# Windowed attention and a low-rank mixer on one core: an MLP in nine chunks of 512 tokens over all batches, attention in its slots

## The chip, the core and the metric

The kernel runs on one core of a Trainium2 chip. The core's engines run in parallel, each through its own queue of instructions in order: TensorE (PE; its weight loads are shown apart, as PEld) multiplies matrices into PSUM, eight banks of 512 float32 columns on 128 partitions; VectorE (DVE) and ScalarE (ACT) do elementwise work and empty PSUM; GpSimd (POOL) does elementwise work in SBUF and here issues all loads; SyncE (SP) issues the stores. Semaphores order the engines among each other. The metric is the device time of one execution in microseconds (us).

## What is computed

```python
# q, k, v: (8, 8, 576, 64) batch, head, token, dimension; U (576, 32), V (32, 576)
# w_ch1 (512, 2048), w_ch2 (2048, 512); all float32
scores = (q @ k.T) / 8, kept where 0 <= i - j < 64, else -1e9
attn   = softmax(scores)                       # per head
x      = attn @ v, heads side by side          # (8, 576, 512)
h      = x.T @ U @ V                           # mixes tokens through rank 32
u      = x + h.T
out    = u + relu(u @ w_ch1) @ w_ch2           # (8, 576, 512)
```

## The kernel before

The operands become bfloat16 in the loads; sums stay float32 in PSUM. Work goes batch by batch. In the attention of one batch (`attention_phases`) heads go in four pairs j, and the 576 tokens in nine blocks of 64, each of which sees 128 keys.

- **T(j)** (L168 to L211): k and q of a pair are transposed by TensorE, five tiles each, into two PSUM buffers (`tp`, pool `ps_sm`). ScalarE copies k into `kt` (L184, L188), VectorE copies q into the block-diagonal `qbd` (L204, L208), whose two halves hold the two heads.
- **S(j)** (L218 to L248): nine matmuls of 128 columns, three to a PSUM tile `sc`; exp on ScalarE (L237, 384 columns), multiplication by a 0/1 mask on VectorE (L243).
- **PV(t, hh)** (L255 to L289): for 128 tokens and four heads, eight matmuls of 65 columns: 64 of v and one of ones, which gives the softmax's sum. The even block of 64 tokens goes to the lower 64 PSUM partitions, the odd one to the upper. A block's 128 keys begin at a multiple of 64, so v is also held shifted by 64 tokens: `vaugB`, written by two VectorE copies (L165, L166) from the loaded `vaugA`. A reciprocal and a multiplication on VectorE (L282, L283) give x.
- **U** (hht, L297) and **V** (mix, L315): x against U, five accumulating matmuls of 512 columns with U padded to 128 columns, a copy on ScalarE (L309); then V against that, five matmuls, and the residual add on VectorE (L326) gives u. Then u is transposed (L341, L344).

The MLP of a batch (`mlp_phases`) has 16 blocks **ch1**, each of 128 hidden columns over 576 tokens: four accumulating matmuls of 512 columns into `psA` (L384) and four of 64 into `psB` (L392), then relu, on ScalarE for even blocks (L400) and on VectorE for odd ones (L407). **ch2** makes 128 tokens of output: 16 matmuls of 512 columns (L467), a residual add on VectorE (L476), a store. Since 576 is 4.5 x 128, an even batch makes four output tiles and the odd one after it five.

Batch 0's attention runs alone; after that batch b's MLP is interleaved with batch b+1's attention in an order written out in `emit_interleaved`, which the framework's scheduler still changes by readiness and due order. All loads are issued on POOL's queue (L134, L138, L144): k and q in ten DMAs of 128 or 64 tokens, v in five, the weights between them. The loads of batch b+2 are put into the queue when batch b's MLP begins, and wait there for their buffers. Eight DMAs of that queue are tracked at a time: a ninth waits for the one eight places before it.

Of the kernel before, what the change touches and what calls it, by code (L numbers as in the profile page):

```python
# [17 lines left out]
def kernel(  # L19
# [11 lines left out]
    nc = tc.nc  # L31
# [7 lines left out]
    NC = (S + P - 1) // P  # L39
    NFULL = S // P  # L40
# [28 lines left out]
    maskall = const.tile([P, NB, 2, W], BF16, name="maskall")  # L69
    nc.vector.memset(maskall[:], 1.0)  # L70
    nc.gpsimd.affine_select(
        out=maskall[:, 0, :, :],
        in_=maskall[:, 0, :, :],
# [7 lines left out]
        out=maskall[:, 1:NB, :, :],  # L81
        in_=maskall[:, 1:NB, :, :],
# [3 lines left out]
        pattern=[[0, NB - 1], [0, 2], [-1, W]],  # L86
# [3 lines left out]
        out=maskall[:, 1:NB, :, :],  # L90
        in_=maskall[:, 1:NB, :, :],
# [3 lines left out]
        pattern=[[0, NB - 1], [0, 2], [1, W]],  # L95
        channel_multiplier=-1,
    )

    w1b = const.tile([P, NDC, F], BF16, name="w1b")
    w2b = const.tile([P, NFC, DM], BF16, name="w2b")  # L100
    ub16 = const.tile([P, NC, P], BF16, name="ub16")
    nc.vector.memset(ub16[:, :, R:P], 0.0)
    vmoe = const.tile([P, S], BF16, name="vmoe")
    nc.vector.memset(vmoe[R:64, :], 0.0)
    nc.vector.memset(vmoe[64:P, :], 0.0)

    def load_weights1():
        nc.gpsimd.dma_start(out=w1b[:], in_=moe_w_ch1.rearrange("(c p) n -> p c n", p=P))
        nc.gpsimd.dma_start(
            out=ub16[:, 0:NFULL, 0:R],  # L110
            in_=moe_U[0 : NFULL * P, :].rearrange("(c p) r -> p c r", p=P),
        )
        nc.gpsimd.dma_start(out=ub16[0:REM, NFULL, 0:R], in_=moe_U[NFULL * P : S, :])
        nc.gpsimd.dma_start(out=vmoe[0:R, :], in_=moe_V[:, :])

    def load_weights2():
        nc.gpsimd.dma_start(out=w2b[:], in_=moe_w_ch2.rearrange("(i p) m -> p i m", p=P))

    qbds = []
    for i in range(2):  # L120
        qbd = qbd_pool.tile([P, HP, NB, 2, W], BF16, name=f"qbd{i}")
        nc.vector.memset(qbd[:], 0.0)
        qbds.append(qbd)

    loaded = {}
    pair_state = {}
# [27 lines left out]
    def attention_phases(b):
        qbd = qbds[b % 2]
        qb16, kb16, vaugA = loaded.pop(b)
        holder = {}
        phases = []

        kt = kt_pool.tile([P, HP, S], BF16, name="kt")  # L160
        vaugB = va_pool.tile([P, NFULL, H, VW], BF16, name="vaugB")

        def prep():
            nc.vector.memset(vaugA[:, :, :, D:VW], 1.0)
# [3 lines left out]
        phases.append(prep)  # L168

        def make_transposes(j):  # L170
            def f():
                tpK = ps_sm.tile([P, NC, P], BF16, name="tp", tag="tp")
                for c in range(NFULL):
                    nc.tensor.transpose(  # L174
                        tpK[:, c, :],
                        kb16[:, c, 2 * j : 2 * j + 2, :].rearrange("p h d -> p (h d)"),
                        ident[:],
                    )
                nc.tensor.transpose(  # L179
                    tpK[:, NFULL, :],  # L180
                    kb16[:, NFULL, 2 * j : 2 * j + 2, :].rearrange("p h d -> p (h d)"),
                    ident[:],
                )
                nc.scalar.copy(  # L184
                    out=kt[:, j, 0 : NFULL * P],
                    in_=tpK[:, 0:NFULL, :].rearrange("p c s -> p (c s)"),
                )
                nc.scalar.copy(out=kt[:, j, NFULL * P : S], in_=tpK[:, NFULL, 0:REM])  # L188

                tpQ = ps_sm.tile([P, NC, P], BF16, name="tp", tag="tp")  # L190
                for c in range(NFULL):
                    nc.tensor.transpose(  # L192
                        tpQ[:, c, :],
                        qb16[:, c, 2 * j : 2 * j + 2, :].rearrange("p h d -> p (h d)"),
                        ident[:],
                    )
                nc.tensor.transpose(  # L197
                    tpQ[:, NFULL, :],
                    qb16[:, NFULL, 2 * j : 2 * j + 2, :].rearrange("p h d -> p (h d)"),
                    ident[:],  # L200
                )
# [289 lines left out]
    def emit_interleaved(att, mlp):  # L491
# [25 lines left out]
        for f in seq:  # L517
            f()
# [51 lines left out]
```

## Time and profile before

| | us |
|---|---|
| median of three runs | 426.8 (424.83 to 428.99) |
| span of the profiled execution | 426.2 |
| TensorE busy in it | 375.3 |
| VectorE, ScalarE, GpSimd busy | 241.3, 137.1, 109.0 |

The profile is of one further execution; its own time is given as its span, from the first to the last instruction. The durations below all come from it. A row's "idle before" is the time the engine waited, with what ended the wait. "PEclk" is the granted clock of TensorE as a share of 2.4 GHz. A busy TensorE row covers the time an instruction is in the array; successive ones overlap, so rates are read from starts.

### The profile page before, as it was taken

Reading aid. Unit: us, or ns where it says so; the run is one execution under the profiler, and the core shown is the slowest. Engines: PE = TensorE matmul, PEld = TensorE weight load, DVE = VectorE, ACT = ScalarE, POOL = GpSimd, SP = SyncE. Lnnn points to the kernel's source line nnn. Section 1 sums busy time; section 2 is a strip of 40 time slices with the busy share of each in tenths; the row PEclk is TensorE's granted clock in tenths of the full one; section 3 lists DMA queues with packets and bytes.
Section 4 is the critical chain, followed back from the end, with each engine's and each line's share of the span. In section 5 each row is a group of like instructions: output and inputs, shape, how many; then the busy total and the mean of one; then the engine's idle time right before and its main releaser. Section 6 shows DMA issues by size and latency. Waiting matters only on the chain.

```text
span 426.2 us, 7410 instructions
## 1 busy us (share of the span) xinstructions
PE 375.3 (88%) x3024; PEld 191.8 (45%) x3024; DVE 241.3 (57%) x638; ACT 137.1 (32%) x361; POOL 109.0 (26%) x134
## 2 busy tenths in 40 slices
PE   0548996999997999889996999979998999999995
PEld 0433652346532455335542455425643455445542
DVE  6376675536745387454775267642776267642433
ACT  1330671026510265114720237203830237213300
POOL 9929549303430043300721006300000000000000
PEclk9965798899996999989998999989999999999999
DMA  8999999913981159811918119361001110011011
GB/s 52 150 193 131 168 157 139 108 49 47 92 55 26 72 57 83 55 43 59 109 11 75 49 52 111 23 60 49 26 2 25 51 50 2 2 51 49 2 49 75
DMA packets 121041, 28.33 MB, mean 66 GB/s; under 512 B 113808, under 2 KB 115888, under 8 KB 121008
## 3 DMA queue, kind: packets, MB, share of 16 engines
q0 software_dynamic: 115760, 18.43, 58.3%
q1 hardware_dynamic: 5248, 9.44, 6.3%
q8 instruction: 23, 0.38, 0.4%
q14 instruction: 10, 0.08, 0.1%
HBM read 36.85 MB, written 9.44 MB: 109 GB/s over the span
## 4 chain that ended last, share of the span: by engine, by line
PE 67%; DMA 10%; DVE 7%; POOL 7%; ACT 6%; issue 2%; DVEq 0%; POOLq 0%
PE psU L467 28%; PE psA L384 21%; DMA vaugA<-in_v_dram 5%; POOL vaugA L144 4%; ACT ptj L237 4%; DMA w1b<-in_moe_w_ch_dram 4%; PE xr L274 3%; PE psB L392 3%; PE sc L229 3%; PE tp L192 2%; PE tp L341 2%; DVE osb L476 2%; PE psA L319 2%; ACT ch1Tp L400 2%; PE tp L174 1%
## 5 line engine op out<-in xcount | busy, mean ns | idle before, releaser
L384 PE MATMUL psA<-uT,w1b 128*128 128x512 bf16 x512 | 143.0, 384 | 0.8 <-ACT uT L349 0.6
L467 PE MATMUL psU<-w2b,ch1Tp 128*128 128x512 bf16 x576 | 137.7, 392 | 0.0
L467 PEld LDWEIGHTS <-ch1Tp 128*128 128x128 bf16 x576 | 56.3, 101 | 66.3 <-issue 9.6
L400 ACT ACTIVATE ch1Tp<-psA 128x512 bf16<-128x512 f32 x64 | 38.2, 597 | 61.7 <-PE psA L384 60.4
L384 PEld LDWEIGHTS <-w1b 128*128 128x128 bf16 x512 | 42.5, 98 | 22.5 <-issue 0.4
L407 DVE TENSOR_SCALAR ch1Tp<-psA 128x512 bf16<-128x512 f32 x64 | 44.1, 689 | 13.6 <-PE psA L384 10.6
L349 ACT COPY uT<-tp 128x512 bf16<-128x512 bf16 x32 | 19.0, 594 | 100.1 <-PE tp L344 100.1
L237 ACT ACTIVATE ptj<-sc 128x384 bf16<-128x384 f32 x96 | 44.0, 495 | 7.1 <-PE sc L229 5.4
L144 POOL DMA_DIRECT2D vaugA<-in_v_dram x40 | 33.8, 875 | 42.2 <-PE psA L384 40.2
L392 PEld LDWEIGHTS <-w1b 128*128 128x128 bf16 x512 | 31.1, 99 | 24.0 <-DVE x_b_503 L283 4.4
L392 PE MATMUL psB<-uT,w1b 128*128 128x64 bf16 x512 | 37.1, 195 | 3.9 <-DVE x_b_503 L283 3.9
L243 DVE TENSOR_TENSOR ptj<-ptj,maskall 128x384 bf16<-128x384 bf16 x96 | 31.3, 354 | 9.6 <-ACT ptj L237 8.3
L184 ACT COPY kt<-tp 128x512 bf16<-128x512 bf16 x32 | 18.8, 588 | 47.8 <-PE tp L179 47.8
L319 PE MATMUL psA<-hhTb,vmoe 128*128 128x512 bf16 (+1 forms) x40 | 17.5, 443 | 18.9 <-DVE osb L476 15.0
L274 PEld LDWEIGHTS <-ptj 128*64 128x64 bf16 x576 | 18.2, 116 | 31.3 <-issue 12.6
L282 DVE RECIPROCAL rcp<-xr 128x4 f32<-128x4 f32 (+1 forms) x80 | 14.1, 179 | 23.2 <-PE xr L274 23.0
L229 PEld LDWEIGHTS <-kt 128*128 128x128 bf16 x288 | 20.6, 100 | 14.3 <-issue 8.8
L274 PE MATMUL xr<-vaugA,ptj 128*64 128x65 bf16 x320 | 21.7, 208 | 0.5 <-DVE ptj L243 0.5
L274 PE MATMUL xr<-vaugB,ptj 128*64 128x65 bf16 x256 | 20.5, 209 | 0.9 <-DVE x_b_161 L283 0.8
L204 DVE COPY qbd_114<-tp 64x512 bf16<-64x512 bf16 x32 | 13.4, 420 | 12.3 <-PE tp L197 12.0
L165 DVE COPY vaugB<-vaugA 64x2304 bf16<-64x2304 bf16 x8 | 7.1, 886 | 23.1 <-DMA vaugA<-in_v_dram 23.0
L309 ACT CAST hhTb<-pshh 128x512 bf16<-128x512 f32 x8 | 4.7, 586 | 41.9 <-PE pshh L302 41.9
(178 smaller groups left out, 415.6 us busy)
## 6 DMA issues: line engine op xcount, KB each, us to landing
out_dram<-osb SPq DMA_DIRECT2D x32, 256.0 KB, 2.0
vaugA<-in_v_dram POOLq DMA_DIRECT2D x32, 128.0 KB, 4.2
w1b<-in_moe_w_ch_dram POOLq DMA_DIRECT2D x1, 2048.0 KB, 15.0
w2b<-in_moe_w_ch_dram POOLq DMA_DIRECT2D x1, 2048.0 KB, 17.2
out_dram<-osb SPq DMA_DIRECT2D x8, 128.0 KB, 2.2
kb_119<-in_k_dram POOLq DMA_DIRECT2D x4, 128.0 KB, 3.9
qb_118<-in_q_dram POOLq DMA_DIRECT2D x4, 128.0 KB, 4.3
vaugA<-in_v_dram POOLq DMA_DIRECT2D x8, 64.0 KB, 3.8
```

The costliest lines, as they stand in the source:

```text
L144: nc.gpsimd.dma_start(out=vaugA[0:rows, c, :, 0:D], in_=v[b, :, c * P : c * P + rows, :].rearrange("h p d -> p h d"),)
L229: nc.tensor.matmul(sc[:, bb, :], kt[:, j, w0 : w0 + P], qbd[:, j, blk, :, :].rearrange("p g q -> p (g q)"), start=True, stop=True,)
L237: nc.scalar.activation(out=ptj[:, prange, :, :], in_=sc[:], func=ACT.Exp, scale=scale,)
L243: nc.vector.tensor_tensor(out=ptj[:, prange, :, :], in0=ptj[:, prange, :, :], in1=maskall[:, prange, :, :], op=ALU.mult,)
L274: nc.tensor.matmul(xr[r0 : r0 + W, hl, 0 : D + 1], pts[j][:, blk, g, :], rhs, start=True, stop=True,)
L319: nc.tensor.matmul(psh[0:mt, :], vmoe[:, t * P : t * P + mt], hhTb[:, :], start=True, stop=True,)
L349: nc.scalar.copy(out=uT[:, dc, 0 : NFULL * P], in_=tpU[:, 0:NFULL, :].rearrange("p c s -> p (c s)"),)
L384: nc.tensor.matmul(psA[:, :], w1b[:, dc, i * P : (i + 1) * P], uT[:, dc, 0:512], start=(dc == 0), stop=(dc == NDC - 1),)
L392: nc.tensor.matmul(psB[:, :], w1b[:, dc, i * P : (i + 1) * P], uT[:, dc, 512:S], start=(dc == 0), stop=(dc == NDC - 1),)
L400: nc.scalar.activation(out=ch1Tp[:, i, colb : colb + 512], in_=psA[:, :], func=ACT.Relu)
L407: nc.vector.tensor_relu(out=ch1Tp[:, i, colb : colb + 512], in_=psA[:, :])
L467: nc.tensor.matmul(psU[0:nrows, :], ch1Tp[:, i, col0 : col0 + nrows], w2b[:, i, :], start=(i == 0), stop=(i == NFC - 1),)
```

## The change

The MLP no longer goes by batches: the 4608 tokens of all batches are nine chunks of 512. A chunk has 32 slots, each of four 512-column matmuls: 16 slots of ch1, one block each, then 16 quarters of ch2, four to an output tile. Chunk c is filled with the attention and mixing of batch c+1, whose pieces have fixed slots (`PLACE`); chunks 7 and 8 have none. The framework's scheduler is off: engines get their instructions in the order written.

In the attention, k and q of a pair are transposed in separate pieces (TK, TQ), into one PSUM buffer (`ps_tp`) in place of two, and each is copied out whole (576 columns). Scores go five and four blocks to a PSUM tile of two banks, so exp and mask have 640 and 512 columns. PV takes all eight heads of 128 tokens in one piece, 16 matmuls. U writes 32 columns per token tile, into four groups of 32 partitions, without padding; V is held four times over so that V's matmul sums the groups. Of the shifted copies of v, that of batch 0 is on VectorE and the others are on POOL. Batches 0 and 1 load k and q grouped by six tokens, 1536 bytes of float32 to a piece, and transpose them in twelve tiles of 96 columns. The start order of POOL's queue is: k and q of batch 0, its v, V, w1 in three parts, w2 in two, k, q and v of batch 1. U comes by SP's queue.

```diff
-    ps_sc = ctx.enter_context(tc.tile_pool(name="ps_sc", bufs=2, space=bass.MemoryType.PSUM))
-    ps_sm = ctx.enter_context(tc.tile_pool(name="ps_sm", bufs=2, space=bass.MemoryType.PSUM))
-    ps_x = ctx.enter_context(tc.tile_pool(name="ps_x", bufs=2, space=bass.MemoryType.PSUM))
+    ps_mm = ctx.enter_context(tc.tile_pool(name="ps_mm", bufs=3, space=bass.MemoryType.PSUM))
     ps_big = ctx.enter_context(tc.tile_pool(name="ps_big", bufs=2, space=bass.MemoryType.PSUM))
+    ps_tp = ctx.enter_context(tc.tile_pool(name="ps_tp", bufs=1, space=bass.MemoryType.PSUM))
...
+    ctx.enter_context(tc.manual_schedule())
...
+    def shift_v(b, eng):
+        va, vb = vA[b % 2], vB[b % 2]
+        eng.tensor_copy(out=vb[0:W, :, :, 0:D], in_=va[W:P, :, :, 0:D])
+        eng.tensor_copy(out=vb[W:P, 0 : NFULL - 1, :, 0:D], in_=va[0:W, 1:NFULL, :, 0:D])
...
-            nc.vector.tensor_copy(out=vaugB[0:W, 0:NFULL, :, :], in_=vaugA[W:P, 0:NFULL, :, :])
-            nc.vector.tensor_copy(out=vaugB[W:P, 0:NFULL, :, :], in_=vaugA[0:W, 1:NC, :, :])
...
+        def TK(j):
+            def f():
+                nc.scalar.copy(out=like(kt[j][:]), in_=tr(kb, j))
...
+        def TQ(j):
+            def f():
+                tp = tr(qb, j)
                 for g in range(2):
                     rs = slice(g * W, g * W + W)
...
+                    nc.vector.tensor_copy(out=like(qbd[j][rs, g, :]), in_=tp[rs])
...
+        def SC(j, part):
+            blks = range(0, 5) if part == 0 else range(5, NB)
...
+                nc.scalar.activation(out=dst, in_=sc[:, 0 : n * P], func=ACT.Exp, scale=scale)
+                mk = maskA[:, 5 - n : 5, :, :].rearrange("p n g w -> p (n g w)")
+                nc.vector.tensor_tensor(out=dst, in0=dst, in1=mk, op=ALU.mult)
...
+        def PV(t):
...
+                xr = ps_big.tile([P, 2, CH], FP32, name="xr", tag="big")
+                for h in range(H):
+                    for blk in blks:
+                        r0 = ((blk + odd) % 2) * W
...
+        def U():
+            ps = ps_big.tile([P, 2, CH], FP32, name="pshh", tag="big")
+            for t in (0, 1, 2, 3, 4):
+                g = t % 4
                 nc.tensor.matmul(
...
+                    ps[g * R : (g + 1) * R, 0, :],
+                    ub[odd][:, t, :],
...
+    PLACE = {
+        "T": [0, 1, 2, 3, 4, 5, 6, 7],
+        "S": [3, 4, 5, 6, 7, 8, 9, 10],
...
+    for c in range(NCH):
+        slots = [[] for _ in range(NSLOT)]
+        if c + 1 < B:
+            shift_v(c + 1, nc.gpsimd)
+            if c + 2 < B:
+                for _ in load_kq(c + 2, False):
+                    pass
+                load_v(c + 2)
+            a = attention(c + 1)
...
+        for fill, extra in zip(mlp(c), slots):
+            fill()
+            for f in extra:
+                f()
```

The other slots are PV 12 to 16, U 18, V 20 to 22, and the transposes of u (UT) 22 to 26.

Three places of the new order follow. VectorE, around the end of a batch's PV, before (`osb` is the residual add of ch2, `u_b` that of the mixing, `vaugB` the shifted v):

```order
L282 RECIPROCAL rcp<-xr 64x4
L283 TENSOR_TENSOR x_b_1116<-xr,rcp 64x256
L165 COPY vaugB<-vaugA 64x2304
L476 TENSOR_TENSOR osb<-psU,u_b_163 64x512
L476 TENSOR_TENSOR osb<-psU,u_b_505 64x512
L326 TENSOR_TENSOR u_b_1118<-psA,x_b_1116 128x512 x4
L326 TENSOR_TENSOR u_b_1118<-psA,x_b_1116 64x512
L166 COPY vaugB<-vaugA 64x2304
```

and now:

```order
L313 RECIPROCAL rcp<-xr 128x8
L314 TENSOR_TENSOR xs_99<-xr,rcp 128x512
L313 RECIPROCAL rcp<-xr 64x8
L314 TENSOR_TENSOR xs_99<-xr,rcp 64x512
L422 TENSOR_TENSOR osb<-psU,un 128x512
L352 TENSOR_TENSOR un<-psv,xs_99 128x512 x4
L352 TENSOR_TENSOR un<-psv,xs_99 64x512
L422 TENSOR_TENSOR osb<-psU,un 128x512 x3
```

The shift copies, which wait for v's load, stood ahead of the adds and are gone from this queue.

VectorE in slots 4 to 9 of a chunk now (`c_5` and so on are ch1's blocks, `qbd` the copies of TQ, `pt` the masks of S):

```order
L286 TENSOR_TENSOR pt_1124<-pt_1124,maskA 128x512
L400 TENSOR_SCALAR c_5_1159<-psA 128x512
L262 COPY qbd_115<-tpn 64x576 x2
L286 TENSOR_TENSOR pt_1169<-pt_1169,maskA 128x640
L286 TENSOR_TENSOR pt_1169<-pt_1169,maskA 128x512
L400 TENSOR_SCALAR c_7_1204<-psA 128x512
L262 COPY qbd_116<-tpn 64x576 x2
L286 TENSOR_TENSOR pt_1214<-pt_1214,maskA 128x640
```

Each relu stands behind the mask of the slot before it, and the copies of TQ behind the relu.

POOL's queue from batch 0's v on, now (`vA` and `vB` are v and its shifted copy, `kg` and `qg` the grouped k and q of batch 1):

```order
L122 DMA vA_101<-in_v_dram 128x8x64 x4
L126 DMA vB_103<-in_v_dram 64x8x64
L200 DMA vrep<-in_moe_V_dram 32x576 x4
L203 DMA w1b<-in_moe_w_ch_dram 128x4x512 x2
L203 DMA w1b<-in_moe_w_ch_dram 128x4x1024
L206 DMA w2b<-in_moe_w_ch_dram 128x8x512 x2
L104 DMA kg<-in_k_dram 96x8x384
L104 DMA qg<-in_q_dram 96x8x384
L122 DMA vA_102<-in_v_dram 128x8x64 x4
L126 DMA vB_104<-in_v_dram 64x8x64
L133 COPY vB_104<-vA_102 64x32x64
L134 COPY vB_104<-vA_102 64x24x64
```

Both weights are now ahead of batch 1's k, q and v; before, w1 was ahead of them and w2 behind them. The two copies are the shift of v.

## Rows read from the trace of the kernel before

**Rows 1.** The page: span, and busy time of TensorE and VectorE with its share.
```profile
span 426.2 us, 7410 instructions
PE 375.3 (88%) x3024; PEld 191.8 (45%) x3024; DVE 241.3 (57%) x638; ACT 137.1 (32%) x361; POOL 109.0 (26%) x134
```

**Rows 2.** Chain that ended last, in order of time: start, us, what.
```profile
43.43 0.59 PE psA L384
...
345.42 0.88 PE psA L384 x4
...
388.84 0.86 PE psA L384 x4
...
403.54 0.86 PE psA L384 x4
404.52 17.28 PE psU L467 x80
421.83 0.68 DVE osb L476
```

**Rows 3.** Timeline around 125 us: start, us, engine, line, operation, [idle before].
```profile
121.01 4.20 POOL L144 DMA_DIRECT2D vaugA<-in_v_dram  x5 [10.05 <-PE psA L384]
...
128.15 0.76 DVE L165 COPY vaugB<-vaugA 64x2304 bf16<-64x2304 bf16 x1 [4.66 <-DMA vaugA<-in_v_dram]
...
130.40 1.30 PE L319 MATMUL psA<-hhTb,vmoe 128*128 128x512 bf16 x2 [3.59 <-DVE osb L476]
```

**Rows 4.** Waits, whole span: us in total, times, longest.
```profile
DVE vaugB L165 <- DMA vaugA<-in_v_dram: 23.0, 6, 4.7
...
PE psA L319 <- DVE osb L476: 15.0, 7, 3.6
```

**Rows 5.** Timeline, TensorE, a T of batch 7 with what follows.
```profile
350.87 0.40 PE L192 MATMUL tp<-ident,qb_3602 128*128 128x128 bf16 x4
351.11 0.22 PE L197 MATMUL tp<-ident,qb_3602 128*128 128x128 bf16 x1
351.16 0.28 PE L392 MATMUL psB<-uT,w1b 128*128 128x64 bf16 x4
```

**Rows 6.** Timeline, TensorE, a PV group between two ch1 matmuls.
```profile
362.31 0.59 PE L384 MATMUL psA<-uT,w1b 128*128 128x512 bf16 x2
...
362.84 0.22 PE L274 MATMUL xr<-vaugB,ptj 128*64 128x65 bf16 x1
362.85 0.22 PE L274 MATMUL xr<-vaugA,ptj 128*64 128x65 bf16 x1
...
363.10 0.39 PE L384 MATMUL psA<-uT,w1b 128*128 128x512 bf16 x1
```

**Rows 7.** Instruction groups: shape, count, busy us, mean ns, idle before.
```profile
L407 DVE TENSOR_SCALAR ch1Tp<-psA 128x512 bf16<-128x512 f32 x64 | 44.1, 689 | 13.6 <-PE psA L384 10.6
...
L400 ACT ACTIVATE ch1Tp<-psA 128x512 bf16<-128x512 f32 x64 | 38.2, 597 | 61.7 <-PE psA L384 60.4 <-ACT kt L188 1.3
...
L243 DVE TENSOR_TENSOR ptj<-ptj,maskall 128x384 bf16<-128x384 bf16 x96 | 31.3, 354 | 9.6 <-ACT ptj L237 8.3
...
L204 DVE COPY qbd_114<-tp 64x512 bf16<-64x512 bf16 x32 | 13.4, 420 | 12.3 <-PE tp L197 12.0
```

**Rows 8.** Stretches: busy us (count) of each engine, granted clock, DMA share, GB/s.
```profile
43.40:47.90 4.50, 4.47 (x30) 3.10 (x30) 2.09 (x3) 2.80 (x9) 4.50 (x5) 0.51 1.06 133
47.90:55.00 7.10, 7.05 (x82) 4.72 (x80) 6.33 (x23) 5.52 (x16) 0.97 (x2) 1.00 1.23 201
```

**Rows 9.** Start: chain row of w1's load; page row of v's loads; timeline of POOL.
```profile
16.83 15.04 DMA w1b<-in_moe_w_ch_dram
...
vaugA<-in_v_dram POOLq DMA_DIRECT2D x32, 128.0 KB, 4.2
...
4.98 1.18 POOL L89 TENSOR_SCALAR_AFFINE_SELECT maskall<-maskall 128x1024 bf16<-128x1024 bf16 x1
```

**Rows 10.** Timeline: the last store's issue.
```profile
423.25 0.33 SPq L483 DMA_DIRECT2D out_dram<-osb  x1
```

More of the change, by code (lines that the diff above doesn't have):

```diff
@@ L71 @@
+    kq0 = load_kq(0, True)
+    next(kq0)
+    next(kq0)
+    make_identity(nc, ident[:])
+    next(kq0)
+    next(kq0)
+    nc.vector.memset(maskA[:], 1.0)
+    for j in range(HP):
+        nc.vector.memset(qbd[j][0:W, 1, :], 0.0)
+        nc.vector.memset(qbd[j][W:P, 0, :], 0.0)
     nc.gpsimd.affine_select(
-        out=maskall[:, 0, :, :],
-        in_=maskall[:, 0, :, :],
+        out=maskA[:, 0, :, :],
+        in_=maskA[:, 0, :, :],
         compare_op=ALU.is_ge,
@@ L94 @@
         base=W,
-        pattern=[[0, NB - 1], [0, 2], [1, W]],
+        pattern=[[0, 4], [0, 2], [1, W]],
         channel_multiplier=-1,
     )
[L99 to L114, printed above, removed]
@@ new lines, with uT_of @@
+    w1v = moe_w_ch1.rearrange("(c p) n -> p c n", p=P)
+    for lo, hi in ((0, 512), (512, 1024), (1024, 2048)):
+        nc.gpsimd.dma_start(out=w1b[:, :, lo:hi], in_=w1v[:, :, lo:hi])
+    w2v = moe_w_ch2.rearrange("(i p) m -> p i m", p=P)
+    for lo, hi in ((0, 8), (8, 16)):
+        nc.gpsimd.dma_start(out=w2b[:, lo:hi, :], in_=w2v[:, lo:hi, :])
+    for _ in load_kq(1, False):
+        pass
+    load_v(1)
+    u_tiles = {}
+    uT_tiles = {}
+    def uT_of(c):
+        if c not in uT_tiles:
+            uT_tiles[c] = uT_pool.tile([P, NDC, CH], BF16, name="uTc")
+        return uT_tiles[c]
@@ new lines, in attention, with tr @@
+    def attention(b):
+        odd = b % 2
+        kb, qb = loaded[b]
+        va, vb = vA[odd], vB[odd]
+        x = xs[odd]
+        g0 = (b * S) // P
+        pcs = {}
+        pts = [None] * HP
+        grouped = b < 2
+        def tr(src, j):
+            if grouped:
+                tp = ps_tp.tile([P, GR, GP], BF16, name="tpg", tag="tp")
+                for c in range(GR):
+                    for g in range(2):
+                        nc.tensor.transpose(
+                            tp[g * D : (g + 1) * D, c, :], src[:, 2 * j + g, c, :], ident[0:GP, 0:GP]
+                        )
+                return tp.rearrange("d c p -> d p c")
+            tp = ps_tp.tile([P, NT, P], BF16, name="tpn", tag="tp")
+            for t in range(NT):
@@ L188, in f @@
[L188 to L201, printed above, removed]
+            return tp.rearrange("d t p -> d (t p)")[:, 0:S]
@@ new lines, in VM @@
+        def VM(ts):
+            def f():
+                ps = ps_big.tile([P, 2, CH], FP32, name="psv", tag="big")
+                for n, t in enumerate(ts):
+                    off = t * P + (0 if odd else W)
+                    nc.tensor.matmul(
+                        ps[:, n, :], vrep[:, off : off + P], hh["sb"][:], start=True, stop=True
+                    )
+                for n, t in enumerate(ts):
+                    g = g0 + t
+                    lo = W if (odd and t == 0) else 0
+                    hi = W if (not odd and t == NT - 1) else P
+                    if g not in u_tiles:
+                        u_tiles[g] = u_pool.tile([P, DM], BF16, name="un")
+                    nc.vector.tensor_tensor(
+                        out=u_tiles[g][lo:hi, :],
+                        in0=ps[lo:hi, n, :],
+                        in1=x[lo:hi, t, :, :].rearrange("p h d -> p (h d)"),
+                        op=ALU.add,
+                    )
+            return f
@@ new lines, in f @@
+                nc.scalar.copy(out=uT_of(g // TPC)[:, :, col : col + P], in_=tp[:])
+            return f
+        pcs["T"] = [f for j in range(HP) for f in (TK(j), TQ(j))]
+        pcs["S"] = [SC(j, a) for j in range(HP) for a in range(2)]
+        pcs["PV"] = [PV(t) for t in range(NT)]
+        pcs["U"] = [U]
+        pcs["V"] = [VM((0, 1)), VM((2, 3)), VM((4,))]
+        pcs["UT"] = [UT(t) for t in range(NT if odd else NT - 1)]
+        return pcs
+    DVE_RELU = (1, 3, 5, 7, 9, 11, 13, 15)
@@ L459, in make_ch2 @@
[L459 to L469 removed]
+                c1[i] = c1_pool.tile([P, CH], BF16, name=f"c1_{i}")
@@ new lines, in f, with ch2 @@
+                if i in DVE_RELU:
+                    nc.vector.tensor_relu(out=c1[i][:], in_=ps[:])
+                else:
+                    nc.scalar.activation(out=c1[i][:], in_=ps[:], func=ACT.Relu)
+            return f
+        acc = {}
+        def ch2(t, quarter):
+            def f():
+                g = c * TPC + t
+                if quarter == 0:
+                    acc[t] = ps_mm.tile([P, DM], FP32, name="psU", tag="mm")
+                for i in range(4 * quarter, 4 * quarter + 4):
+                    nc.tensor.matmul(
+                        acc[t][:],
+                        c1[i][:, t * P : (t + 1) * P],
@@ new lines, in f @@
+                    nc.sync.dma_start(out=outf[g * P : (g + 1) * P, :], in_=osb[:])
+            return f
+        return [ch1(i) for i in range(NFC)] + [ch2(t, r) for t in range(TPC) for r in range(4)]
+    PLACE = {
+        "T": [0, 1, 2, 3, 4, 5, 6, 7],
+        "S": [3, 4, 5, 6, 7, 8, 9, 10],
+        "PV": [12, 13, 14, 15, 16],
+        "U": [18],
+        "V": [20, 21, 22],
+        "UT": [22, 23, 24, 25, 26],
+    }
+    ORDER = ("T", "S", "PV", "U", "V", "UT")
+    a = attention(0)
+    for j in range(HP):
+        a["T"][2 * j]()
+        a["T"][2 * j + 1]()
+        if j > 0:
+            a["S"][2 * j - 2]()
+            a["S"][2 * j - 1]()
@@ new lines @@
+    a["S"][6]()
+    a["S"][7]()
+    shift_v(0, nc.vector)
+    for i in range(2):
+        nc.vector.tensor_copy(out=ub[i][:], in_=uf[i][:])
+    for part in ("PV", "U", "V", "UT"):
+        for f in a[part]:
+            f()
+    for c in range(NCH):
[4 more added lines that the diff above has]
+                for _ in load_kq(c + 2, False):
+                    pass
+                load_v(c + 2)
+            a = attention(c + 1)
+            for part in ORDER:
+                for f, s in zip(a[part], PLACE[part]):
+                    slots[s].append(f)
+        for fill, extra in zip(mlp(c), slots):
+            fill()
+            for f in extra:
+                f()
```

510 lines of the change are left out of this document (161 added, 349 removed).

## The prediction

> **What bounds the kernel now.** I read the busy times first: TensorE is busy 88% of the span, VectorE 57% [rows 1]. So TensorE is the resource that everything is scheduled around, and the question is where it is not fed. Next the chain of waits, merged by line, as a clock of the loop [rows 2]: batch 0's MLP starts at 43.43, batch 6's at 345.42, batch 7's at 388.84. Batch 6 (attention of batch 7 inside it, four output tiles) takes 43.4 us and loses no time to loads. An odd batch has a fifth output tile, 17.28/5 = 3.45 us, so its clean length is 46.9. Six batches from 43.43 to 345.42 took 302.0 us; clean they would take 3 x 43.4 + 3 x 46.9 = 270.9. So 31 us are lost in the first six batches. The waits say to what: VectorE waited 23.0 us in six pieces for v's DMA, and TensorE 15.0 us in seven pieces for the residual add behind it [rows 4]. The timeline of one piece shows the mechanism [rows 3]: POOL issues v only when its buffer comes free (121.01, five DMAs in 4.20 us), VectorE reaches the half-tile shift copy L165 and sits 4.66 us, and the add and mixing behind it are late, so TensorE idles 3.59. The rest of the 31 is the low clock at the start, 4.5 us at 0.51 [rows 8], worth 2.3, and the clock that falls again after such waits.
>
> **What the change does to each part.**
>
> *MLP.* Before, a block of ch1 is four 512-column matmuls in 0.86 and a block's pitch is 0.98 with the four 64-column ones [rows 2]; 128 blocks cost 125.4. Now 9 x 16 blocks of 0.86 cost 124.2. ch2 keeps 576 matmuls at 17.28/80 = 0.216. A chunk alone is 32 slots x 0.863 = 27.6 us. Taken by itself, this part gains 1 us.
>
> *Attention inside a chunk, TensorE time.* Five transposes take 0.29 (350.87 to 351.16, where the next matmuls start) [rows 5], 0.058 for 128 columns; a score block has 128 columns too: T 8 x 0.29 = 2.3, S 36 x 0.058 = 2.1, the transposes of u 18 x 0.058 = 1.0, V 5 x 0.216 = 1.1. PV: before, eight matmuls in two column halves, with the switch in and out, take 0.36 (363.10 - 362.31, less two psA of 0.216) [rows 6], ten such groups a batch. Now there are four groups of sixteen and one of eight; a group of sixteen lies between 0.36 and 0.72, I take 0.55, as the switch is paid once: 2.6 in place of 3.6. U now has 32-column tiles in four column groups, which no row shows. If four run side by side, as the two halves do in [rows 6], U is two matmuls' time and a switch, 0.65; one after another it is 1.1 to 1.3. I take 0.65. Sum 9.7.
>
> *Waits inside a chunk.* There is now one buffer for transposed tiles, so each T waits for the copy of the T before it, and both copying engines work in order. An even slot: relu 0.60 and a 576-column copy of some 0.65 (0.597 x 576/512 at most) on ScalarE; an odd one: relu 0.69 and two copies of at most 0.47 (0.42 x 576/512) on VectorE [rows 7]; each starts about 0.2 after the matmul. TensorE has 1.15 (slots 0 to 2) or 1.4 (slots 3 to 7, with scores) to cover them. That leaves waits of about 0.3, 0.5, 0.05 and 0.35 ahead of slots 1 to 4. From slot 4 a longer chain closes: K copy 0.65, exp of 512 columns 0.6, mask 0.47 (0.354 for 384 columns, times 512/384 [rows 7]), the next relu, which stands behind that mask on VectorE, 0.69, two copies 0.94, with T and hand-overs 0.55: 3.9 us for two slots against 2.8 of TensorE work. It closes once fully: 1.0. I take 2.0 per chunk, between 0 and 4 x 1.1 = 4.4. PV, V and u's transposes have a slot of 0.86 or more each for 0.9 of VectorE or 0.6 of ScalarE, and two buffers or slots between them; nothing there waits. A chunk with attention: 27.6 + 9.7 + 2.0 = 39.3.
>
> *The v wait.* The shift copy leaves VectorE for POOL, whose queue holds only loads behind it. v for the batch after next is issued after slot 16, lands some 8 us later (4.20 of issuing, 4.2 to landing [rows 3, 9]), and is needed in slot 12 of the chunk after: over 30 us of cover. The osb add and the mixing no longer stand behind a load. I count all of its 29 us (31 less the 2.3) as gone. A copy on POOL is priced by its nearest row, a select of 1024 elements in 1.18 [rows 9]: 2048 and 1536 elements, 4.1 us a batch, off the path. While they run (slots 24 to 30) VectorE has only adds that read PSUM; only in chunk 0 can they fall on masks. The Trainium skill speaks against this move: "SBUF — State Buffer", section "Who interferes with whom", says that GpSimd and VectorE share one pair of SBUF ports, and that a VectorE instruction with both inputs in SBUF, as the mask multiply has, contends with a GpSimd instruction that reads SBUF. No row of this trace has a POOL copy to show it; by that rule the sum would grow by up to 4.1 in chunk 0.
>
> *The start.* Attention of batch 0 runs first as before; its U and V no longer wait for weights, since V lands ahead of w1. It should be done at 35 to 39. But batch 1's k and q now stand behind w1 and w2 in the DMA queue, and slots 0 and 1 of chunk 0 need them. w1 was issued at 16.83 and took 15.04, so it landed at 31.9 [rows 9]; now it is issued about as late, say it lands at 31. Then w2, 2.1 MB, and k and q, 0.59 MB each, at the 0.2 MB/us that weights got (201 GB/s written, [rows 8]): 10.5 + 5.9, q landing at 47.4. Bounds: 44 (w1 two us earlier, small lags) to 50 (packets of 768 B at 150 GB/s). So TensorE waits some 9 us, the start gains nothing, and the clock is low again when work resumes: 2.3 as before [rows 8]. Batch 1's transposes are twelve of 96 columns, not five: 1.0 more for the eight.
>
> *The sum.* 47.4 (two blocks and one T done) + rest of chunk 0: 39.3 - 2.0 + 2.3 + 1.0 = 40.6; six chunks 235.8; two alone 55.2; tail: one add of 0.69 and the 2.95 from the last issue at 423.25 to the end [rows 10], 3.7. Total **382.7 us**, say 383, against a profiled span of 426.2 (0.6 under the median of 426.8). Set against the old loop: 29 from v, 7 from PV, 4 from U, some 6 from fewer waits in each batch, and 2 given back at the start.
>
> **Rivals.**
> - *Copies lengthen the chain (slower than before).* Place: slots 0 to 10, VectorE. If its relu, copies and masks took twice my rates (576 columns, 640-column masks and a busy POOL have no row), the pair of slots goes from 3.9 to 5.9: 2 x 1.5 + 2 x 2.0 + 1.5 in slots 8 to 10 = 8.5 a chunk, 60 in all: 443. It decides from 44/7 = 6.3 us a chunk, some 1.75 times my rates. For it: VectorE is at 57% now and loses no work but the shift copies. Against: mask, copy and relu rows scale gently, and relu is unchanged. Chance 0.10, of which 0.03 lands near no change.
> - *More waits, U in series.* U at 1.3 (+4.5 over seven batches) and 1.5 more wait a chunk (+10.5): 398. Chance 0.15.
> - *Fewer waits.* k and q land at 44 (-3.4) and T's waits nearly vanish (-1.4 a chunk, -10): 370. For it: ScalarE and VectorE overlap consecutive instructions a little, which I left out. Chance 0.12.
> - *POOL's copies hold up the masks in every chunk*, being late and running in slots 3 to 10: 4.1 us of VectorE, seven times, all on the chain: 383 + 28 = 411. POOL's order, with v's loads after slot 16, speaks against it. Chance 0.05. (This is the contention that the Trainium skill states in the section named above.)
> - The forecast, 373 to 392: chance 0.58.
>
> **The numbers.** The likeliest is 383. Leaving out the slower case, the POOL case and the ends of the middle ones, 367 to 401 holds about 8 in 10. One per cent (4.3 us) is about what these runs can tell from no change. Faster by more: 0.58 + 0.15 + 0.12 + 0.05 = 0.90; same 0.03; slower 0.07.
>
> **What would show it.** Right: no VectorE wait on v; TensorE idle on batch 1's q until 44 to 50 and then never over 1.5 us; chunks of 38 to 41 us, the two last 27.6 each; waits of T on copies adding up to 1 to 3 us a chunk. Wrong: chunks over 44 us with VectorE busy in slots 3 to 10 (first rival), masks longer where POOL copies run (fourth), U's five matmuls over 1 us (second), or the first T of batch 1 long after its data.

## The result, and the profile after

The changed kernel takes **391.7 us** (median of four runs, 391.0 to 391.7) against 426.3: ratio 0.917, 95% interval 0.913 to 0.921. The forecast was 383, with 367 to 401. The profiled execution has a span of 389.9. In the page, which answers to [rows 1], TensorE's share is the same 88%, of a shorter span: it is busy 32 us less.

```profile
span 389.9 us, 6452 instructions
PE 342.9 (88%) x2672; PEld 173.8 (45%) x2672; DVE 201.6 (52%) x383; ACT 128.0 (33%) x213; POOL 122.5 (31%) x142
```

The chain of waits, as in [rows 2], is again the clock of the loop. Each run of 20 or 24 psU matmuls ends a chunk:

```profile
51.92 1.86 PE psA L391 x4
...
92.41 4.32 PE psU L413 x20
96.73 0.86 PE psA L391 x4
...
130.44 5.18 PE psU L413 x24
135.62 0.86 PE psA L391 x4
...
330.99 13.81 PE psA L391 x64
...
358.62 13.81 PE psA L391 x64
372.43 13.83 PE psU L413 x64
```

Chunk 0 takes 44.8 us (51.92 to 96.73), chunks 1 to 6 together 234.3, 39.04 each, the two without attention 27.6 each. The waits of TensorE and VectorE have another picture than [rows 4]. VectorE's wait for v in every batch is gone; two waits of the start are new, one of TensorE and one of VectorE, and T's waits for VectorE's copies are left:

```profile
PE tpg L236 <- DMA w1b<-in_moe_w_ch_dram: 16.2, 1, 16.2
PE tpn L242 <- DVE qbd_115 L262: 4.9, 6, 0.9
...
DVE vA_101 L192 <- DMA vrep<-in_moe_V_dram: 13.6, 1, 13.6
```

VectorE's timeline at the start explains both. A memset of v's column of ones (L192) is written behind v's load into the same tile, so it waits for that DMA, and the first copy of q (`qbd_113`) stands in order behind it. The row names the load of the weight V (`vrep`) as the releaser, but that load is written behind the memset and can't hold it; v's own four DMAs, issued from 8.68 to 12.20, took 5.2 to 6.9 us to land, and the memset runs when they have landed. e1 below tests this reading.

```profile
18.50 0.09 DVE L192 MEMSET vA_101<- 128x32 bf16 x1 [13.56 <-DMA vrep<-in_moe_V_dram]
...
21.31 1.46 DVE L262 COPY qbd_113<-tpg 64x576 bf16<-64x576 bf16 x2
```

TensorE has one buffer for transposes, and so it idles 16.2 us; the releaser named in its row, w1b, is not what it needs there. Batch 1's q was issued at 21.76 and took 23.9 to land, so it lay ready at 45.7, ahead of its transposes at 56.16. The first transposes of k, which had landed near 42.3, ran at 53.72. Two later ch1 blocks are shown for use below:

```profile
21.76 0.80 POOL L104 DMA_DIRECT2D qg<-in_q_dram  x1
...
qg<-in_q_dram POOLq DMA_DIRECT2D x1, 576.0 KB, 23.9
...
53.72 0.69 PE L236 MATMUL tpg<-ident,kg 96*64 96x96 bf16 x12
...
56.16 0.65 PE L236 MATMUL tpg<-ident,qg 96*64 96x96 bf16 x12
56.74 1.04 PE L391 MATMUL psA<-uTc,w1b 128*128 128x512 bf16 x4
...
74.04 1.02 PE L391 MATMUL psA<-uTc,w1b 128*128 128x512 bf16 x4 [0.87 <-DVE c_9_760 L400]
```

### The profile page after: what moved, and what is told of

The parts are those of the page before. It is cut to its first block, busy times and chain, and to the rows that moved or that the text cites. A ratio compares the mean times of both kernels' runs of the same rounds, so it can differ in the third digit from the quotient of the medians.

```text
span 389.9 us, 6452 instructions
## 1 busy us (share of the span) xinstructions
PE 342.9 (88%) x2672; PEld 173.8 (45%) x2672; DVE 201.6 (52%) x383; ACT 128.0 (33%) x213; POOL 122.5 (31%) x142
## 4 chain that ended last, share of the span: by engine, by line
PE 76%; DVE 12%; ACT 4%; DMA 3%; POOL 2%; issue 2%; ACTq 0%; DVEq 0%; POOLq 0%
PE psU L413 32%; PE psA L391 27%; PE xr L304 3%; PE tpn L242 3%; PE sc L276 3%; PE tpu L365 2%; PE psv L343 2%; DVE qbd_115 L262 2%; DVE qbd_113 L262 2%; DMA w1b<-in_moe_w_ch_dram 2%; PE tpg L236 2%; DMA vA_101<-in_v_dram 1%; PE pshh L328 1%; DVE xs_99 L314 1%; DVE qbd_116 L262 1%
## 5 line engine op out<-in xcount | busy, mean ns | idle before, releaser
L391 PE MATMUL psA<-uTc,w1b 128*128 128x512 bf16 x576 | 143.9, 383 | 1.5 <-DVE c_9_760 L400 0.9
L391 PEld LDWEIGHTS <-w1b 128*128 128x128 bf16 x576 | 51.6, 98 | 48.3 <-issue 3.1
L422 DVE TENSOR_TENSOR osb<-psU,un 128x512 f32<-128x512 f32 x36 | 24.9, 692 | 85.1 <-PE psU L413 85.1
L369 ACT COPY uTc<-tpu 128x512 bf16<-128x512 bf16 x36 | 21.1, 586 | 48.0 <-PE tpu L365 48.0
L236 PE MATMUL tpg<-ident,kg 96*64 96x96 bf16 x96 | 4.8, 254 | 24.4 <-DMA w1b<-in_moe_w_ch_dram 16.2
L113 POOL DMA_DIRECT2D kn_106<-in_k_dram x15 | 13.1, 871 | 36.1 <-PE tpn L242 36.1
L113 POOL DMA_DIRECT2D kn_105<-in_k_dram x15 | 13.1, 870 | 29.6 <-PE sc L276 18.0
L365 PEld LDWEIGHTS <-un 128*128 128x128 bf16 x144 | 11.6, 102 | 11.4 <-issue 3.8
L365 PE MATMUL tpu<-ident,un 128*128 128x128 bf16 x144 | 14.8, 229 | 2.0 <-ACT uTc L369 2.0
L122 POOL DMA_DIRECT2D vA_102<-in_v_dram x16 | 14.2, 912 | 6.0 <-DMA w1b<-in_moe_w_ch_dram 3.7
L352 DVE TENSOR_TENSOR un<-psv,xs_99 128x512 bf16<-128x512 f32 (+1 forms) x20 | 12.6, 682 | 4.2 <-PE psv L343 4.2
L122 POOL DMA_DIRECT2D vA_101<-in_v_dram x16 | 14.3, 954 | 0.0
L314 DVE TENSOR_TENSOR xs_100<-xr,rcp 128x512 bf16<-128x512 f32 (+1 forms) x20 | 13.8, 692 | 0.7
L314 DVE TENSOR_TENSOR xs_99<-xr,rcp 128x512 bf16<-128x512 f32 (+1 forms) x20 | 13.8, 690 | 0.7
L352 DVE TENSOR_TENSOR un<-psv,xs_100 128x512 bf16<-128x512 f32 (+1 forms) x20 | 12.7, 685 | 2.5 <-PE psv L343 2.4
L113 POOL DMA_DIRECT2D qn_108<-in_q_dram x15 | 13.1, 876 | 1.0 <-PE tpn L242 1.0
L113 POOL DMA_DIRECT2D qn_107<-in_q_dram x15 | 13.1, 876 | 0.6 <-PE tpn L242 0.6
```

The source lines that it names most:

```text
L113: nc.gpsimd.dma_start(out=dst[0:rows, t, :, :], in_=src[b, :, t * P : t * P + rows, :].rearrange("h p d -> p h d"),)
L122: nc.gpsimd.dma_start(out=va[:, t, :, 0:D], in_=v[b, :, t * P : (t + 1) * P, :].rearrange("h p d -> p h d"),)
L236: nc.tensor.transpose(tp[g * D : (g + 1) * D, c, :], src[:, 2 * j + g, c, :], ident[0:GP, 0:GP])
L314: nc.vector.tensor_tensor(out=x[lo:hi, t, :, :].rearrange("p (a h) d -> p a h d", a=2), in0=xv[:, :, :, 0:D], in1=rcp[lo:hi].to_broadcast( ...
L352: nc.vector.tensor_tensor(out=u_tiles[g][lo:hi, :], in0=ps[lo:hi, n, :], in1=x[lo:hi, t, :, :].rearrange("p h d -> p (h d)"), op=ALU.add,)
L365: nc.tensor.transpose(tp[:, dc, :], u_tiles[g][:, dc * P : (dc + 1) * P], ident[:])
```

## The experiments

Starts, chunk 0 and the mean of chunks 1 to 6 are read from each run's TensorE timeline and chain; e5 is a variant of the kernel before. Each ratio is to the kernel before on the same chip. The means of e1 and e2 hold one longer chunk each, chunk 1 (40.5 and 39.8), in which masks ran beside GpSimd's copies: two masks took 3.81 in e1.

| run | us | ratio (95%) | chunk 0 starts | chunk 0 | chunks 1 to 6 |
|---|---|---|---|---|---|
| changed kernel | 391.7 | 0.917 (0.913 to 0.921) | 51.9 | 44.8 | 39.04 |
| e1 memsets early | 383.2 | 0.900 (0.896 to 0.904) | 38.4 | 48.1 | 39.31 |
| e2 e1, k and q of batch 1 before w2 | 377.9 | 0.887 (0.884 to 0.890) | 37.5 | 44.1 | 39.20 |
| e3 two transpose buffers | 372.6 | 0.874 (0.871 to 0.878) | 44.4 | 42.1 | 37.43 |
| e4 shift on VectorE | 390.8 | 0.917 (0.914 to 0.920) | 51.2 | 43.4 | 39.07 |
| e5 kernel before, third v buffer | 412.2 | 0.966 (0.963 to 0.969) | | | |
| e6 e2 and e3 | 361.2 | 0.847 (0.845 to 0.850) | 32.1 | 43.4 | 37.31 |
| e7 e6, shift on VectorE | 376.2 | 0.882 (0.879 to 0.884) | 31.7 | 57.4 | 37.31 |
| e8 PV in halves | 401.0 | 0.940 (0.937 to 0.942) | 52.5 | 45.9 | 40.18 |
| e9 U in one column group | 400.3 | 0.940 (0.936 to 0.943) | 52.8 | 45.8 | 40.32 |
| e10 e6, v of batch 1 before w2 | 362.6 | 0.851 (0.847 to 0.854) | 32.0 | 42.6 | 37.57 |
| e11 e6, shift on VectorE from batch 2 | 361.2 | 0.848 (0.844 to 0.852) | 32.7 | 42.6 | 37.31 |
| e12 e2 without e1 | 390.5 | 0.917 (0.913 to 0.920) | 51.9 | 44.3 | 39.04 |

**e1: the memsets ahead of the loads.**

```diff
+    for i in range(2):
+        nc.vector.memset(vA[i][:, :, :, D:VW], 1.0)
+        nc.vector.memset(vB[i][:, :, :, D:VW], 1.0)
     load_v(0)
 ...
-        nc.vector.memset(vA[i][:, :, :, D:VW], 1.0)
-        nc.vector.memset(vB[i][:, :, :, D:VW], 1.0)
```

> The four VectorE memsets of the columns of ones in vA and vB are written ahead of batch 0's v loads instead of behind them; nothing else moves. Theory A (the start is late because these memsets wait for v's DMA, 13.6 us, and the first copies of q stand behind them on VectorE): the first copy of q runs at 7 to 9 us instead of 21.3, chunk 0's first ch1 block at about 38 instead of 51.9, then TensorE waits for batch 1's q, which lands at about 46. The second slot goes from 55.5 to about 47, so 392 becomes 382 to 385. Rival B (the start is bound by loading: v, w1 and batch 1's k and q): the first ch1 block moves, but the time stays within 2 us of 391.7.

383.2, theory A. In TensorE's timeline the first ch1 block starts at 38.39 instead of 51.92, and then batch 1's k and q are the limit, at 43.03 and 46.27, each with the wait in brackets:

```profile
38.39 1.86 PE L392 MATMUL psA<-uTc,w1b 128*128 128x512 bf16 x4 [0.67 <-ACT uTc L370]
43.03 0.69 PE L237 MATMUL tpg<-ident,kg 96*64 96x96 bf16 x12 [2.78 <-DMA kg<-in_k_dram]
...
46.27 0.69 PE L237 MATMUL tpg<-ident,qg 96*64 96x96 bf16 x12 [0.73 <-DMA qg<-in_q_dram]
```

**e2 and e12: the order of POOL's queue,** with and without e1.

```diff
+    for _ in load_kq(1, False):
+        pass
     w2v = moe_w_ch2.rearrange("(i p) m -> p i m", p=P)
 ...
-    for _ in load_kq(1, False):
-        pass
     load_v(1)
```

> The memsets moved as in the run before, and in POOL's queue the k and q of batch 1 ahead of w2. Theory A (once the memsets no longer hold the start, the loads of batch 1's k and q behind w2 are its next bound): k and q land before 38 us, chunk 0 starts at about 38 and has no wait of TensorE over 2 us, and the total is 391.7 - 14 = 378, 375 to 380 with less time at the low clock. Rival B (the start is bound by the attention of batch 0 itself or by w1): no more than 1 us below the run with the memsets alone. Rival C: w2 is late then, and slots 16 to 24 of chunk 0 wait for it.

> The changed kernel with batch 1's k and q ahead of w2, and the memsets left behind batch 0's v. Theory A (in the changed kernel TensorE never waited for batch 1's q, which landed at 45.7, six us before chunk 0 began; the order of the queue matters only once the memsets are out of the way): 390 to 392. Rival B (the start is shortened by earlier k and q in any case): 388 or less.

377.9 and 390.5, theory A both times. With e1 the new order is worth 5.3 us; without it chunk 0 still starts at 51.9, and the order gives 1.2 of 391.7 at most: the ratio to the kernel before is the same 0.917. Here the late load became a cost only when the work was ready for it.

**e3: two buffers for transposes.**

```diff
-    ps_mm = ctx.enter_context(tc.tile_pool(name="ps_mm", bufs=3, space=bass.MemoryType.PSUM))
+    ps_mm = ctx.enter_context(tc.tile_pool(name="ps_mm", bufs=2, space=bass.MemoryType.PSUM))
-    ps_tp = ctx.enter_context(tc.tile_pool(name="ps_tp", bufs=1, space=bass.MemoryType.PSUM))
+    ps_tp = ctx.enter_context(tc.tile_pool(name="ps_tp", bufs=2, space=bass.MemoryType.PSUM))
```

> Two PSUM banks for transposed tiles in place of one, two for the MLP's accumulators in place of three. Theory A (the waits in slots 0 to 7, 1.7 to 1.9 us a chunk, come from the single buffer): they go, 7 x 1.7 = 12 us, and the total is about 380; if half of them come back as waits for a free accumulator, 386. Rival B (the waits come from the in-order queues of VectorE and ScalarE, and the third accumulator is what covers late relus): waits before ch1 blocks take their place, and the total is 391 to 400.

372.6, below theory A. The chunks lose 1.6 us each, as expected: slot 6 of the changed kernel (first fence) waits 0.79, that of e3 (second) not at all. The rest is the start: chunk 0 begins 7.6 earlier, since the transposes of two pairs are made while VectorE is held, and is 2.7 shorter.

```profile
144.11 1.03 PE L391 MATMUL psA<-uTc,w1b 128*128 128x512 bf16 x4
145.92 0.45 PE L242 MATMUL tpn<-ident,kn_106 128*128 128x128 bf16 x5 [0.79 <-DVE qbd_115 L262]
```

```profile
131.83 1.03 PE L391 MATMUL psA<-uTc,w1b 128*128 128x512 bf16 x4
132.69 0.44 PE L242 MATMUL tpn<-ident,kn 128*128 128x128 bf16 x5
```

The price of the lost accumulator is small: 16 ch1 blocks without attention take 14.44 in e6 instead of 13.81.

**e6: both causes removed.** The edits of e1, e2 and e3 together.

> The start of the second run (memsets early, k and q of batch 1 ahead of w2) and the two transpose buffers of the third together. Theory A (two separate causes, the start and the waits in slots 0 to 7, whose gains add up but for what both take from batch 0's attention): six chunks 1.4 us shorter, chunk 0 about 3, batch 0's attention 2 to 4: 377.9 - 8.4 - 3 - 3 = 363.5, 361 to 366. Rival B (they are one cause: most of what two buffers gave was at the start): 370 or more.

361.2, theory A: start and transposes are separate causes. With e11 it is the fastest version.

**e4, e7, e11: which engine shifts v.** e4 is the changed kernel with the first added line of the diff, e7 is e6 with it, e11 is e6 with the second.

```diff
-            shift_v(c + 1, nc.gpsimd)
+            shift_v(c + 1, nc.vector)
 ...
+            shift_v(c + 1, nc.gpsimd if c == 0 else nc.vector)
```

> The shift copies of v for batches 1 to 7 on VectorE instead of GpSimd, at the same place of the program (the start of a chunk). Theory A (it is the early load that took the 29 us of waiting away, and the engine matters little): no VectorE wait for v in chunks 1 to 6; VectorE has 0.70 + 0.56 us more per chunk ahead of slot 0, of which between none and all reaches TensorE, less some 2 us of slower masks beside GpSimd's copies in chunk 0: 390 to 400. Rival B (the move to GpSimd is what removed the wait): VectorE waits for v in every chunk again, some 4 us each, and the total is over 410.

> The run before it in this list with the shift copies of batches 1 to 7 on VectorE. Theory A (GpSimd's copies lengthen VectorE's masks where both run at once, in chunks 0 and 1, by 1.6 to 2.9 us, and elsewhere the engine makes no difference): masks of 0.49 and 0.43 everywhere, total within 3 us below the run before it. Rival B (with the transpose waits gone nothing is left to cover VectorE's 1.26 us per chunk): 7 x 1.26 = 9 us slower than the run before it.

> The run e6 with the shift copies of batch 1 on GpSimd and those of batches 2 to 7 on VectorE. Theory A (the 15 us that the run with all of them on VectorE lost are one wait, VectorE's 19.6 us for batch 1's v in chunk 0 with everything in order behind it): that wait is gone and the rest costs nothing, 359 to 362. Rival B (VectorE's 1.26 us per chunk counts, since the transposes have no slack left): 6 x 1.26 = 7.6 us more, 367 to 370.

e4: no change. VectorE's only wait for v is now that of chunk 0:

```profile
DVE vB L133 <- DMA vA<-in_v_dram: 3.6, 1, 3.6
```

So in chunks 1 to 6 it is the early load, with the copy at the start of a chunk, that took the waiting away, and not the engine. e7 lost 15 us, which neither theory had. Its chunks 1 to 6 have the length of e6; all of it is in chunk 0, where VectorE's timeline shows one wait for batch 1's v:

```profile
49.59 0.70 DVE L133 COPY vB<-vA 64x2048 bf16<-64x2048 bf16 x1 [19.55 <-DMA vA<-in_v_dram]
```

e11 confirms it: with that one copy back on GpSimd, 361.2. So with the early start of e6 the move to GpSimd matters for one batch, whose v lands after work that is ready.

**e5: the kernel before with a third buffer for v.**

```diff
-    va_pool = ctx.enter_context(tc.tile_pool(name="va", bufs=2))
+    va_pool = ctx.enter_context(tc.tile_pool(name="va", bufs=2)); vl_pool = ctx.enter_context(tc.tile_pool(name="vl", bufs=3))
 ...
-        vaugA = va_pool.tile([P, NC, H, VW], BF16, name="vaugA")
+        vaugA = vl_pool.tile([P, NC, H, VW], BF16, name="vaugA")
```

> The kernel before, with three buffers for the loaded v in place of two, so that GpSimd issues v's five DMAs one batch earlier; the code is else unchanged (the framework's scheduler moves a few instructions). Theory A (the 31 us lost in the old loop are VectorE's wait for v, with the low clock behind it): VectorE has no wait for v after batch 0, an even and an odd batch take 43.4 and 46.9 us, and the total is 426 - 29 = 397, 395 to 400. Rival B (the wait moves to k and q, or the shift copies hold the add and the mixing in any case): less than half of it goes, 412 or more.

412.2: 14 us, Rival B's number, but not its mechanism. VectorE's wait for v fell from 23.0 [rows 4] to this:

```profile
DVE vaugB L165 <- DMA vaugA<-in_v_dram: 4.2, 3, 2.6
```

The chains, before (first fence) and of e5 (second), show each batch's last output tiles; a start plus its length ends a batch:

```profile
93.75 3.45 PE psU L467 x16
...
142.77 6.91 PE psU L467 x32
...
193.98 3.45 PE psU L467 x16
...
242.29 6.91 PE psU L467 x32
...
293.30 3.45 PE psU L467 x16
...
337.95 6.91 PE psU L467 x32
```

```profile
41.21 16.28 DMA w2b<-in_moe_w_ch_dram
...
62.97 5.61 DMA vaugA<-in_v_dram
...
93.07 3.45 PE psU L467 x16
...
139.38 6.91 PE psU L467 x32
...
187.01 3.45 PE psU L467 x16
...
231.86 6.91 PE psU L467 x32
```

Before, batches 1 to 4 took 52.5, 47.8, 51.8 and 47.6; batch 5, without a wait for v, 48.1, and batch 6 44.0. Against 48.1 and 44.0 the four lost 15.4. In e5 they take 49.8, 44.2, 48.3 and 44.0. Batch 0 took 53.8 before (43.43 to 97.20), 9.8 over 44.0, and still ends at 96.52 in e5. The chain's first two rows put that down to batch 1's v, which stands behind w2 in the queue; it was not tried alone, and that it is the cause is not shown.

**e8: PV in ten pieces of eight matmuls.**

```diff
-        def PV(t):
+        def PV(t, a):
 ...
-                for h in range(H):
+                for h in range(4 * a, 4 * a + 4):
 ...
-        "PV": [12, 13, 14, 15, 16],
+        "PV": [11, 12, 13, 14, 15, 16, 17, 18, 19, 20],
 ...
```

> The changed kernel with PV in ten pieces of eight matmuls (four heads each), as before, in slots 11 to 20 (U in 22, V in 23 to 25, the transposes of u in 25 to 29). Theory A (every group in a slot of its own pays the switch between 512-column and 64-partition matmuls once, so a batch's PV takes 3.6 us in place of 2.3): each chunk is 1.0 to 1.4 us longer and the total 8 to 10 us, some 400. Rival B (the switch costs nothing, a group of sixteen is just twice a group of eight): within 2 us of 391.7.

401.0, theory A. TensorE's timeline gives the price of a group of eight: 156.51 - 155.30, less the 0.86 of the four psA, is 0.35. Groups of sixteen in the changed kernel have a pitch of 1.35, so 0.49. By these prices ten groups of eight cost 3.5 and the changed kernel's groups 2.3, which is the 1.1 that a chunk grew.

```profile
155.30 1.04 PE L391 MATMUL psA<-uTc,w1b 128*128 128x512 bf16 x4
156.26 0.32 PE L304 MATMUL xr<-vA,pt 128*64 128x65 bf16 x4
156.51 1.04 PE L391 MATMUL psA<-uTc,w1b 128*128 128x512 bf16 x4
```

**e9: U in one column group.**

```diff
-                    ps[g * R : (g + 1) * R, 0, :],
+                    ps[0:R, 0, :],
 ...
-                        ps[:, n, :], vrep[:, off : off + P], hh["sb"][:], start=True, stop=True
+                        ps[:, n, :], vrep[0:R, off : off + P], hh["sb"][0:R, :], start=True, stop=True
```

> The changed kernel with U's five matmuls all written to the same 32 partitions, adding up in one group, in place of four groups of 32 partitions; the copy and V's matmul then use these 32 rows only. Theory A (in the changed kernel four column groups run side by side, 0.53 us for the five, and one after another they would take 5 x 0.216 = 1.08 and the switches): 0.55 to 0.7 us more per batch, eight batches, 396 to 397. Rival B (matmuls of 32 columns of weights are quick by themselves): within 1.5 us of 391.7.

400.3, more than either theory. U itself is as theory A has it: 1.18 (163.70 to 164.88) against 0.53 in the changed kernel (160.60 to 161.13), 0.65 more. The first fence is the changed kernel, the second e9:

```profile
160.60 0.60 PE L328 MATMUL pshh<-xs_100,ub_97 128*32 128x512 bf16 x5
161.13 0.39 PE L413 MATMUL psU<-w2b,c_12_1755 128*128 128x512 bf16 x1
```

```profile
163.70 1.25 PE L328 MATMUL pshh<-xs,ub 128*32 128x512 bf16 x5
164.88 1.90 PE L413 MATMUL psU<-w2b,c 128*128 128x512 bf16 x8
166.71 0.60 PE L343 MATMUL psv<-hh,vrep 32*128 32x512 bf16 x2
167.25 1.04 PE L413 MATMUL psU<-w2b,c 128*128 128x512 bf16 x4
...
```

The other 0.6 per chunk is V, which the edit made 32 rows deep: a pair takes 0.54 (166.71 to 167.25; 0.43 before the edit), and the four psU behind it 0.97 (0.87).

**e10: batch 1's v ahead of w2 too.**

```diff
+    load_v(1)
     w2v = moe_w_ch2.rearrange("(i p) m -> p i m", p=P)
 ...
-    load_v(1)
```

> The run e6 (361.2) with batch 1's v ahead of w2 as well. Theory A (chunk 0's last wait is the 1.8 us of PV for GpSimd's shift copies, which stand behind v at 49.5): v lands near 40, the wait goes, 359 to 360, less up to 1.5 if the copies then run beside masks. Rival B (w2 becomes late: its second half lands after slot 18 of chunk 0, near 58 us): 362 or more.

362.6: Rival B's number, but not for w2's sake, which nothing waits for. PV's wait is gone and chunk 1 starts 1.0 earlier (74.5 against 75.5), but chunk 1 takes 38.8 instead of 37.2: GpSimd's copies of batch 2 now run beside a mask, which takes 2.03 instead of 0.43, and TensorE then waits 1.55 for the relu behind it:

```profile
81.98 0.43 DVE L287 TENSOR_TENSOR pt<-pt,maskA 128x512 bf16<-128x512 bf16 x1 [1.09 <-ACT pt L285]
...
84.77 2.03 DVE L287 TENSOR_TENSOR pt<-pt,maskA 128x512 bf16<-128x512 bf16 x1 [0.28 <-ACT pt L285]
```

```profile
84.63 1.89 POOL L133 COPY vB<-vA 64x2048 bf16<-64x2048 bf16 x1 [5.83 <-DMA vA<-in_v_dram]
```

```profile
87.58 1.02 PE L392 MATMUL psA<-uTc,w1b 128*128 128x512 bf16 x4 [1.55 <-DVE c L401]
```

## Why the prediction was right, and where it was off

The direction, the mechanism of the new loop and the sums of all parts but the start came out, one of them by luck; the whole was 7 us short in the span, 8.7 in the median.

- **The start: the step that failed.** "It should be done at 35 to 39" overlooked that the memsets of v's ones stand behind v's load in program order, and that VectorE's queue holds q's copies behind them. Batch 0's attention ended at 51.9, and the transposes of batch 1's q, forecast at 47.4, ran at 56.2: 8.8 late. TensorE never waited for batch 1's q; the prediction's own sign of being wrong came instead, the first T of batch 1 long after its data (53.72, with k landed near 42.3). e1 takes the memsets' wait alone away, and what the step said follows: done at 38.4, then waits for k (2.78) and q (0.73) until 46.3, 383.2 in all against 383. What I had called the limit, q behind w1 and w2, became one only there (e2 against e12).
- **The rest of chunk 0,** forecast 40.6, took 40.6 (56.16 to 96.73), but the equality is luck. The forecast had 2.3 of slow clock in it; in the changed kernel the two slow blocks stand ahead of 56.16, and the one at 56.74 already runs in 1.04. In their place came what the sum left out: the two VectorE copies of batch 1's grouped q take 1.51 (0.91 for the later batches, 0.94 forecast), so T waits longer, and the relu behind two long masks held TensorE 0.87 at 74.04. Six chunks: 235.8 forecast, 234.3 measured. The two alone: 55.2 and 55.3. Tail: 3.7 and 3.6.
- **Inside a chunk.** Attention 9.7 and waits 2.0 were forecast. The changed kernel has 39.04 - 27.62 = 11.4 for both, and e3 takes 1.6 of waits away. PV 0.49 a group (0.55 forecast) and U 0.53 (0.65) were near; e8 and e9 show that both widths are real gains, some 9 us, and 8 x 0.65 = 5 us.
- **"I count all of its 29 us as gone" was mis-sized,** though it stood only in the comparison with the old loop and not in the sum. v's wait cost 15.4 in batches 1 to 4. Of the 31 us, 9.8 were batch 0, and 5.4 came from clean lengths taken too short (43.4 and 46.9 in place of 44.0 and 48.1, three of each). So the 36.3 us between the spans are: v 15.4, clean work 25.5 (357.7 before, from 4 x 44.0 + 3 x 48.1 + 37.4; 332.2 now, from 7 x 39.04 + 55.3 + 3.6), 4.0 less excess in the first batch (9.8, now 5.8), less 8.5 for the later start, which is 36.4. I had credited clean work with 17, so in that comparison two errors, 29 for v's wait and 17 for clean work, partly cancel.
- **The rivals.** Copies did not lengthen the chain of chunks 1 to 6, U was not in series, and POOL's copies held masks in chunk 0 alone: two masks took 2.52 instead of 0.92 (0.49 and 0.43), and the next two 1.36. In e4, with no copy on GpSimd, the first two take 0.83, and chunk 0 is 1.4 shorter. The rule of the Trainium skill ("SBUF — State Buffer", section "Who interferes with whom"), that a VectorE instruction with two inputs in SBUF contends with GpSimd reading SBUF, agrees with the row of 2.52, and with e10's of 2.03.

```profile
70.74 2.52 DVE L286 TENSOR_TENSOR pt_732<-pt_732,maskA 128x640 bf16<-128x640 bf16 x2
```

```profile
70.97 2.02 POOL L133 COPY vB_103<-vA_101 64x2048 bf16<-64x2048 bf16 x1 [5.16 <-DMA vA_101<-in_v_dram]
```

What stays open: of the 25.5 us of clean work e8 and e9 show PV and U, some 14; the rest, some 11, was not taken apart. The 9.8 of batch 0 before has no run of its own.

## What to carry to other kernels

When a change writes out its own order, walk each engine's queue from the first instruction and ask of every small one what it waits for: a 0.09 us memset behind a DMA cost 8.5 us here, and the releaser that the trace named for TensorE was not the cause. Size a recurring loss from a clean period of the same kind, and test it by taking away its cause in the kernel before. Late loads, single buffers and busy queues hide each other: the order of the loads gave at most 1 us alone and 5 once the memsets were out of the way.

## What the runs showed of the hardware

- A mask (128x512, bf16, both inputs in SBUF) that takes 0.43 on VectorE took 2.03 beside GpSimd's copy in e10, more than that copy's whole 1.89.
- GpSimd needs 1.89 us for a copy of 64x2048 bf16 that VectorE does in 0.70.
- U's five matmuls of 512 columns in four groups of 32 columns take 0.53 with the switches, in one group 1.18 (e9).
- After the thin work of batch 0 the first ch1 blocks start 1.80 apart for four matmuls (51.92 to the next T at 53.72), about half the later pace. The row of that stretch (columns as in [rows 8]) gives the granted clock as 1.00 (the level of 2.4 GHz), where the kernel before had 0.51 (that of 1.2 GHz) at the same place, so here the rows leave open why the pace is half. In e6 the first block already takes 1.02, at 32.10.

```profile
51.90:56.70 4.80, 4.78 (x32) 1.85 (x31) 0.43 (x1) 1.24 (x2) 4.80 (x5) 1.00 0.51 33
```
